# Five engine queues in a new searched order, with register reads as tasks of their own

## The chip, the core and the metric

The kernel runs on one core of a Trainium2 chip. A core has five engines that run side by side, each with an instruction queue that it works off strictly in order: TensorE (PE in the profile, its weight loads apart as PEld), VectorE (DVE), ScalarE (ACT), GpSimd (POOL) and SyncE (SP), which here issues most DMAs. An instruction that waits for another engine holds everything behind it in its own queue. The metric is device time in microseconds (us) of one execution; less is better.

## What is computed

Block-sparse attention (4 batches, 8 heads, 768 positions, head size 64) and then a feed-forward layer with a squared relu on its result:

```python
scores = scale * np.matmul(q, k.transpose(0, 1, 3, 2))
mask = np.abs(blk_i - blk_j) <= window
mask = mask | (blk_i == 0) | (blk_j == 0) | (blk_i == n_blocks - 1) | (blk_j == n_blocks - 1)
for qb in range(n_blocks):
    for kb in sampled_blocks[qb]:
        mask[qb * block:(qb + 1) * block, kb * block:(kb + 1) * block] = True
scores = np.where(mask, scores, -1000000000.0)
attn = np.exp(scores - np.max(scores, axis=-1, keepdims=True))
attn = attn / (np.sum(attn, axis=-1, keepdims=True) + 1e-09)
attn_out = np.matmul(attn, v)
...
h = x @ w_in
r = np.maximum(h, 0.0)
g = r * r
return (g @ w_out).astype(np.float32)
```

x is the attention's output as 3072 rows of 512; w_in is 512 x 2048 and w_out 2048 x 512. A block has 32 positions, there are 24 blocks, and each block of queries sees its neighbours, the first and the last block, and three blocks drawn at random that are only known when the kernel runs.

## The kernel before

Two heads make a unit (u), so there are 16 units, four to a batch. Batches 0 and 1 are computed dense: `scores`, then `exps` on ACT, `masks` on DVE (a product with a 0/1 tile) and `values` on PE, for 256 queries and two key chunks at a time. Batches 2 and 3 are computed sparse, in six visits (v) of two query groups (g) each: `k_gather` copies the keys of the sampled blocks together (on POOL or DVE), `v_gather` and `v_window` fetch their value rows by DMA, and `s_scores`, `s_exps`, `s_masks`, `s_values`, `s_normalize` follow. `s_transp` or `x_transp_dma` turn the result into the x tile of the feed-forward layer. There, `hidden` makes 1024 columns of h in four parts on PE, `relu` (ACT or DVE) and `square` (ACT, or POOL) follow, and `output` multiplies by w_out in eight parts; `out_copy` and `store` bring the result out. `cast_qk` and `cast_v` turn loaded values into bf16 on DVE or POOL.

All of this is cut into some 1200 tasks. A task names the tasks that it depends on (`deps`), the buffers that it takes (`get`) and those that it gives back (`put`); a buffer may be taken again when all who hold it have put it. The string `PROGRAM` is a list of words such as `V120`, `G73` or `P84/1`: the engine (P, V, A, G, S for PE, DVE, ACT, POOL, SP), the task's number and, for tasks that take one of the four PSUM cells X, the cell. `run_program` goes through the words and issues each task's instructions on the engine named. So the string sets which engine does a task and the order in each engine's queue, and nothing else does; waits between engines follow from deps and buffers.

Where the block numbers are needed as addresses (`k_gather`, and `v_gather` where SP issues it), they have to be in registers of the engine that uses them. `blocks_of` (line 559) reads the six numbers of a group with one register load, `load_blocks(e)` (line 569) does it for every group that the program gives to engine e, and `table_rows` (line 523), a short DVE task, calls it for POOL, DVE and SP at once. A `v_gather` on POOL is one indirect DMA (line 579); on SP it is six DMAs with addresses from registers (line 582).

An x tile (pool xT, four buffers) is read by four `hidden` groups of a tile of 256 tokens; before, it is put by the last part of the group with the highest column numbers.

Of the kernel before, what the change touches and what calls it, by code (L numbers as in the profile page):

```python
# [25 lines left out]
def kernel(  # L26
# [14 lines left out]
    nb = S // block  # L41
# [7 lines left out]
    NF = d_ff // P  # L49
# [733 lines left out]
    def T_(f, *args, **kw):  # L783
        return Task((lambda e: f(*args, e)), **kw)
# [146 lines left out]
    tb, mk_claims, mk_buf = {}, [], {}  # L931
# [6 lines left out]
    tb["slots"] = T_(table_slots, deps=[t, p], get=tmp)  # L938
    hb = Buf("X")
# [4 lines left out]
    for us in [range(b * HP, (b + 1) * HP) for b in range(B)]:  # L944
# [11 lines left out]
        if us[0] >= SB * HP:  # L956
            b = us[0] // HP
# [8 lines left out]
    for T in TILES:  # L966
# [3 lines left out]
        for f in range(0, NF, n_u):  # L970
# [31 lines left out]
        A29 G35 P4/3 V32 P30/0 P12/2 P14/3 P9/1 P5/1 V31 P33/1 V111 P36/3 P0/2 A37 V1 V34 P102/2 V209 V46 P47/0 P106/1 A103 V48 P104/3  # L1002
        V43 A107 P44/0 G57 P7/2 V45 A105 P58/1 V54 P113/0 V59 P55/2 A114 P117/3 G41 V56 P2/1 V67 A118 P115/2 V3 P108/0 A116 V64 P127/1
        V109 P10/3 P65/3 A128 P123/2 V66 A124 P68/1 P125/3 G75 V69 V63 P92/1 P110 A126 P133/2 G76 V112 A134 P137/3 G52 S28 S42 S18 S19
        V93 S20 P88/0 A138 G38 V155 V89 P84/1 P119/2 G74 V85 A60 P86/0 P39/3 P135/1 V120 G73 A87 V40 A136 P121 P61/0 G49 P129/3 V122
        V62 G77 V70 P176/2 P170/0 P139/1 A177 G81 V130 G80 A171 V140 P146/2 P131 V132 A147 P149/3 V172 P71/0 P141 V142 A150 V72 P50/2
        P173/1 V148 P781/0 A174 P782 V178 P189/3 P783 V51 A190 V175 P90/1 P15/2 P96/2 P784 V91 A97 P183/3 V151 A785 P94/2 P179/1 V95
        A184 G787 P143/0 P774/2 V180 P775 A144 V191 G78 P186/3 P181 P776 V182 A187 P777 V145 P157/0 V778 A786 P152/3 A158 P160/1 V188
        P788/2 A161 V153 P163/0 P789 V185 A164 P790 V162 P154 P217/1 P791 A156 V159 A218 P192/0 V165 P795/3 A792 V193 S82 P166/1 S83
        V296 V219 S53 S254 A779 G794 S253 P194 P100/2 A780 P796 V195 V167 A101 P214/0 P797 G793 A215 P168 P798 V169 P211/2 V799 P824/1  # L1010
        G79 A212 P825 P196/0 G256 V216 P826 A197 P199/3 P818/2 G801 S257 P827 A200 P819 V828 P202/0 A800 S261 P228/3 P820 G22 A203
        S262 P821 V213 P812/1 S269 A229 V822 P813 G258 P220/0 A829 P814 V201 P245/2 S259 P221 A246 V198 P815 P802/3 V222 A816 P231/2
        V266 P223 P803 A232 V204 S267 P239/1 V230 P804 A224 A240 V264 S270 P242/0 P205/2 V233 S265 A243 P225/1 P206 P805 V207 A226
        S277 V274 P288/0 S436 S255 P208 P806 V227 A289 S275 V247 P11/1 P291/1 A823 P234/0 V241 P807 A292 V210 V244 P98/2 P235 V272
        P808 A99 V236 A817 S273 P298/2 V290 P248/1 P237 A299 P809 V238 S278 V293 P285/0 S279 V300 P249 A810 P830/2 V250 P831 A286 V282
        P304/3 P251 P832 V260 A305 P301/0 V252 P833 S263 V287 P852/1 A302 S334 S283 V834 P853 P846/3 G280 P313/0 V303 P854 A314 P316/2
        S281 P855 P847 A317 V856 G284 P294/0 P848 A835 S271 P295 V306 P310/1 S21 P849 G268 V297 A311 P864/2 V318 P865 S440 A850 P307/0
        V315 P866 S438 A857 P308 G851 S446 P355/3 P867 V309 A356 P322/1 V868 P858/0 P859 A323 P349/3 V357 P325/2 P860 A350 V312 P861
        P836/1 V276 A326 V351 S456 P319/3 A862 P328/2 V327 S439 P320 S447 A329 V321 P352/0 P837 S811 V324 A353 S454 P339/2 V330 P838
        A340 V354 P331/3 P342/0 A869 S385 V341 P332 P358/2 V333 P839 A343 V23 S335 G441 P359 A863 P336/3 P361/0 G443 P840 A337 P841  # L1020
        G451 A362 S622 P364/3 G449 P842 A365 P373/0 G445 S450 P843 A374 G461 P870/3 A844 S444 P367/0 V338 P871 A368 V344 S463 P872
        V347 V360 S455 V366 S442 P376/0 P345/1 A377 V363 P379/2 P346 P873 S452 V348 A380 V369 P403/0 P874 A404 V375 S464 P370/2 V378
        P400/1 P393/0 V381 P371 A401 P875 V372 S471 S448 A394 V402 P382/1 P390/2 V405 P383 A391 P387/0 P876 V384 A388 V395 S386 P406/1
        P886/2 V392 A407 P887 V457 P427/0 P877 A428 V465 P24/1 P888 S497 S462 A878 G453 P889 V408 S458 P880/0 A890 P881 P430/3 S466
        P882 V27 G891 A431 P883 P409/2 A884 P926/3 V26 P927 A885 P410 G469 P415/0 V398 V25 P928 V411 G467 A416 P892/1 S608 V389 P424/2
        S879 P893 A425 P929 S468 V432 P894 A930 P895 V426 P396/0 S470 A896 P16/2 V429 P898/3 S845 P397 S616 A931 P418/2 P433/1 V399
        P899 V459 A419 P932/0 P933 V474 S460 P412/2 P900 A413 P901 V417 P934 A902 S473 P434 V420 P935 V435 P482/3 G903 P904/2 A483
        V936 A897 P492/1 P905 V414 A493 P914/3 G503 P915 P480/0 S499 S623 P421/1 A481 P916 S542 P422 P906 G472 V423 V484 P907 S437
        G937 P917 P487/1 P908 V918 A488 P477/1 P490/0 P909 G501 A478 V504 A491 P485/1 P920/3 A919 G543 V494 P921 V479 V621 P475/0 P910
        A486 G500 V489 V625 A476 P911 V613 P495/1 A912 G546 S632 S913 V547 P511/2 S607 P505/0 V496 P922 A512 S520 S502 P923 A506  # L1030
        P954/1 V924 G627 P955 P514/2 P508/0 P956 A515 V507 G524 P557/3 S545 P957 V513 A509 P948/2 A925 P949 S614 P938/0 G544 A558 S498
        P939 V516 A958 V525 P551/3 S523 P950 A552 P940 V510 P554/3 P951 A555 P548/1 P941 G589 S628 A549 P517/3 A952 P966/1 G959 V518
        A953 P967 P535/2 P942 V550 S519 A536 P529/3 P943 G521 S626 V559 P526/2 P944 V590 G522 A527 P945 V537 P968 V609 A946 P960/2
        P961 V556 A530 P969 V528 P532/0 P962 A970 S540 S615 V553 P963 S585 G586 S624 P988/3 A971 V964 P989 P560/1 A533 V531 P990 A965
        V534 P594/2 P994/0 V561 A595 P995 P991 G567 S562 P996 A992 P538/1 V619 V568 S631 A993 P597/3 P972/2 S606 V539 A598 P997 V596
        S541 P600/1 P973 A601 G587 P1000/3 A998 V617 S620 P974 G999 P975 S610 P572/1 P1001 A573 S630 P982/0 G637 P1002 S588 P1003
        P575/1 P983 V1004 A576 P976 V611 P984 P578/1 P569/3 P985 V629 S612 A570 P977 V599 A986 V633 P978 S563 G565 S618 A579 V602
        P1034/3 A1005 P591/0 G635 V574 S634 P979 A592 P1035 G564 S638 P1028/1 A980 V593 P1036 S566 V580 P1029 A987 P1037 P1030 S639
        S636 V1038 P603/2 P1022/0 V604 P1023 P643/3 P1031 V577 P1024 V571 A1032 P1006/2 V642 S641 A644 P1025 G1033 P1007 V1026 P655/3
        P648/1 P1008 A656 S947 A649 P650/3 P1009 S583 S667 G640 A1039 P581/1 A1027 G671 P645/0 P1010 V582 A651 A646 P658/3 V657 G668  # L1040
        P1011 S584 V652 A659 V672 P653/1 P1012 S605 V647 P660/0 P1016/3 A661 G692 P1017 S688 A654 V662 P1013 P1018 V693 P1019 P663/0
        A1020 A1014 P679/3 P1050/1 V664 S731 S665 S981 A680 P682/2 P1051 S1015 A683 P1062/0 S734 P1063 A1021 V684 P676/3 P1052 S751
        S691 P673/2 A677 P1053 G714 P1064 A674 V1054 P1065 P1040/3 A1066 G669 V715 S670 P1041 A1055 G1067 P700/0 V678 P1042 A701
        P697/1 P1056/2 A698 S690 P694/0 P1043 G689 A695 V681 P1057 P1068/1 V699 P719/0 P1069 V696 A720 P1058 V675 P1070 P1071 S666
        P703/0 P1059 A1072 P1044 V1060 P1045 G1061 P685/2 P716/1 P1046 V686 A704 S710 G711 A717 P1047 V702 S687 G757 A1073 P722/2 G712
        P1074/0 A723 V705 P1075 V1048 P706/2 P725/3 P1076 V707 S753 G754 S713 A726 P1077 V721 G733 V724 S756 P1084/2 V718 P1085 V758
# [42 lines left out]
```

## Time and profile before

| | us |
|---|---|
| median of 3 runs | 259.88 |
| lowest and highest run | 258.5, 267.15 |
| the profiled execution | 258.88 |
| its span on the core | 257.1 |

The profile is of one execution. Its span runs from the first to the last instruction; the 1.8 us between span and time lie outside the instructions. For every instruction it has engine, source line, tiles, start and length, and for idle time before it, which engine's signal ended the wait. The granted TensorE clock was 1.00 in every stage. A tile name such as `X<-xT,w_in_sb` is output, arrow, inputs. An engine's name with a q (DVEq, SPq) is its sequencer: register loads, and the issue of DMAs. In a row of a group stand the count, the busy time, the mean in ns, and the idle time before it with what ended it.

### The profile page before, as it was taken

To read this page: it belongs to the slowest core of one execution; us is meant where nothing else is said; L and a number is where in the kernel's file an instruction comes from. 1 tells how busy PE (TensorE), PEld (TensorE's weight loads), DVE (VectorE), ACT (ScalarE), POOL (GpSimd) and SP (SyncE) were. 2 spreads that over 40 slices of the span, in tenths; PEclk is the share of its full clock that TensorE was granted. 3 is DMA by queue.
4 is the path that set the end of the run, shared out by engine and by line. 5 is a ranking of instruction groups with operands and counts; after the bars stand their busy time and mean duration, and the time that the engine had idled before them with its cause. 6 is when DMAs were issued, how large, how long until landed. Compare 5 with 4: busy or idle time off the path is not lost.

```text
span 257.1 us, 12061 instructions
## 1 busy us (share of the span) xinstructions
PE 243.1 (95%) x5265; PEld 182.1 (71%) x5265; DVE 171.3 (67%) x408; ACT 183.6 (71%) x217; POOL 98.8 (38%) x178
## 2 busy tenths in 40 slices
PE   7888999999999997998998999999999999999993
PEld 4667879678874677975864867866875677767683
DVE  7778988899889995969916756657536725730301
ACT  3899999998999797846783975675965286623640
POOL 3183247003316026198556314264357620412100
PEclk9999999999999999999999999999999999999999
DMA  6999989999999996999699779998474923044022
GB/s 200 374 250 207 206 205 155 270 202 252 250 281 179 197 202 153 340 229 154 188 243 202 194 174 167 251 214 199 129 206 95 189 40 60 5 121 148 23 86 83
DMA packets 64692, 47.08 MB, mean 183 GB/s; under 512 B 31567, under 2 KB 60624, under 8 KB 64640
## 3 DMA queue, kind: packets, MB, share of 16 engines
q1 hardware_dynamic: 58512, 37.82, 64.7%
q0 software_dynamic: 5440, 8.05, 16.8%
q8 instruction: 41, 0.67, 1.1%
q10 hardware_dynamic: 688, 0.46, 0.6%
q14 instruction: 11, 0.09, 0.1%
HBM read 35.51 MB, written 7.91 MB: 169 GB/s over the span
## 4 chain that ended last, share of the span: by engine, by line
PE 53%; DVE 5%; DVEq 1%; issue 1%; ACT 1%; ACTq 0%
PE X L203 49%; PE X L653 4%; DVE VB L123 1%; ACT pT L623 1%; DVEq L561 1%; DVE MKS L123 1%; DVE pT L630 1%; DVE r L709 0%; DVE KG L599 0%; DVE qc L123 0%; DVE XS L413 0%; DVE KG L593 0%; DVE XS L662 0%; DVEq L599 0%; DVE rs L410 0%
## 5 line engine op out<-in xcount | busy, mean ns | idle before, releaser
L203 PE MATMUL X<-xT,w_in_sb 64*128 64x256 bf16 x1536 | 100.8, 269 | 2.8 <-issue 1.5
L203 PE MATMUL X<-w_out_sb,g 64*128 64x512 bf16 (+3 forms) x960 | 95.2, 334 | 0.1
L203 PEld LDWEIGHTS <-w_in_sb 64*128 64x128 bf16 x1536 | 74.6, 94 | 16.0 <-issue 5.4
L360 ACT ACTIVATE pT<-X 128x1024 bf16<-128x1024 f32 x72 | 70.6, 1030 | 7.6 <-PE X L203 6.8
L623 ACT ACTIVATE pT<-X 128x768 bf16<-128x768 f32 (+1 forms) x56 | 41.6, 766 | 26.5 <-PE X L203 23.9
L203 PEld LDWEIGHTS <-g 64*128 64x128 bf16 x960 | 40.3, 94 | 26.3 <-PE X L203 0.4
L720 POOL TENSOR_TENSOR g<-r 128x1024 bf16<-128x1024 f32 (+1 forms) x20 | 31.6, 1587 | 64.4 <-ACT r L707 47.2
L707 ACT ACTIVATE r<-X 128x1024 f32<-128x1024 f32 x28 | 29.8, 1068 | 20.6 <-PE X L203 20.5
L709 DVE TENSOR_SCALAR r<-X 128x1024 f32<-128x1024 f32 x20 | 24.5, 1224 | 26.7 <-PE X L203 13.7
L367 DVE TENSOR_TENSOR pT<-pT,VG 128x1024 bf16<-128x1024 bf16 x60 | 40.9, 715 | 0.2
L718 ACT ACTIVATE g<-r 128x1024 bf16<-128x1024 f32 (+1 forms) x40 | 35.2, 899 | 2.7 <-DVE r L709 2.5
L203 PE MATMUL X<-QKT 64*128 64x256 bf16 (+1 forms) x384 | 31.6, 250 | 3.3 <-DVE XS L413 1.3
L630 DVE TENSOR_TENSOR pT<-pT,MKS 128x768 bf16<-128x768 bf16 (+1 forms) x48 | 27.6, 607 | 10.7 <-ACT pT L623 10.5
L203 PEld LDWEIGHTS <-QKT 64*128 64x128 bf16 x384 | 16.7, 95 | 9.5 <-issue 4.1
L579 POOL DMA_INDIRECT VG<-rows,idx x19 | 20.2, 1061 | 4.4 <-issue 2.6
L203 PEld LDWEIGHTS <-pT 64*128 64x128 bf16 x768 | 16.0, 94 | 1.9
L203 PE MATMUL X<-VB,pT 64*128 64x65 bf16 x768 | 17.1, 190 | 0.0
L203 PEld LDWEIGHTS <-KG 64*128 64x128 bf16 x528 | 13.8, 95 | 4.5 <-issue 0.2
L659 DVE RECIPROCAL ss<-X 128x8 f32<-128x8 f32 x12 | 2.5, 206 | 19.5 <-PE X L653 17.3
L653 PEld LDWEIGHTS <-pT 128*64 128x64 bf16 x624 | 11.9, 111 | 4.9 <-issue 3.7
L203 PE MATMUL X<-QKT,KG 64*128 64x64 bf16 x528 | 15.3, 190 | 0.1
L123 POOL CAST VB<-vs 128x768 bf16<-128x768 f32 x9 | 7.8, 869 | 16.5 <-DMA vs<-in_v_dram 16.4
(107 smaller groups left out, 210.3 us busy)
## 6 DMA issues: line engine op xcount, KB each, us to landing
vs<-in_v_dram SPq DMA_DIRECT2D x14, 384.0 KB
ks<-in_k_dram SPq DMA_DIRECT2D x13, 384.0 KB
qs<-in_q_dram SPq DMA_DIRECT2D x12, 384.0 KB
out_dram<-ys SPq DMA_DIRECT2D x9, 512.0 KB
VG<-rows SPq DMA_DIRECT2D x20, 132.0 KB
w_in_sb<-in_moe_w_in_dram POOLq DMA_DIRECT2D x4, 512.0 KB, 8.6
w_out_sb<-in_moe_w_out_dram POOLq DMA_DIRECT2D x4, 512.0 KB, 9.9
rows<-VB SPq DMA_DIRECT2D x2, 792.0 KB
```

The source lines that it names most:

```text
L123: (V if e == "DVE" else G).tensor_copy(out=out, in_=in_)
L203: last = nc.tensor.matmul(out(r ^ crossed), lhsT(r ^ crossed, rows), rhs(r ^ crossed, rows), skip_group_check=True, **kw)
L360: A.activation(out=pT[:, :, 0:n], in_=stile.pop(a)[:, :, 0:n], func=AF.Exp, scale=scale)
L367: V.tensor_tensor(out=pT, in0=pT, in1=m[:, None].broadcast_to([P, 2, len(cs), w]), op=AOP.mult)
L579: G.indirect_dma_start(out=to[0:RS * HB], out_offset=None, in_=pairs, in_offset=bass.IndirectOffsetOnAxis(ap=idx[0:RS * HB, g - 1:g], axis=0))
L623: A.activation(out=pT[:, :, 0:n], in_=stile.pop((u, v, gs))[:, :, 0:n], func=AF.Exp, scale=scale)
L630: V.tensor_tensor(out=pT, in0=pT, in1=m[:, None].broadcast_to([P, 2, n]), op=AOP.mult)
L653: nc.tensor.matmul(po[i * D:(i + 1) * D, h, a * VW:(a + 1) * VW], pts[g][:, h, c * D:(c + 1) * D], val, start=a == 0 and c == 0, stop=c == ...
L707: A.activation(out=to, in_=src, func=AF.Relu)
L709: V.tensor_scalar(out=to, in0=src, scalar1=0.0, scalar2=None, op0=AOP.max)
L718: A.activation(out=g, in_=r, func=AF.Square)
L720: (G if e == "POOL" else V).tensor_mul(out=g, in0=r, in1=r)
```

## The change

Three edits of code and a new table.

- `table_rows` no longer reads block numbers. `load_blocks(g0, g1, e)` is a task of its own, two for each of POOL, DVE and SP: groups 0 to 3, and the others. Each depends on `table_slots`, which writes the table that is read, and is placed by the program like any other task.
- The x tile is put by the last part of each of its four `hidden` groups, so it is free when all four are done, in whatever order they stand.
- `PROGRAM` is another string, with six more words. Work moves between engines too: ten `cast_qk` from DVE to POOL, seven `square` from ACT to POOL (six of 1024 columns, one of 512), two `relu` from DVE to ACT, five `v_gather` from POOL to SP, one `mask_evac` and one `x_evac` from ACT to DVE and one `evac` (a copy to QKT) the other way. PE has the same tasks.

```diff
@@ table_rows @@
         V.tensor_scalar(out=idx, in0=low[1][:, P:P + GR], scalar1=float(HB), scalar2=lane, op0=AOP.mult, op1=AOP.add)
-        load_blocks("POOL")
-        load_blocks("DVE")
-        load_blocks("SP")
@@ load_blocks @@
-    def load_blocks(e):
-        for g in wanted[e]:
+    def load_blocks(g0, g1, e):
+        for g in [g_ for g_ in wanted[e] if g0 <= g_ < g1]:
             if g not in held_at[e]:
                 held_at[e][g] = blocks_of(g, ENGINE[e])
@@ the list of tasks @@
     tb["slots"] = T_(table_slots, deps=[t, p], get=tmp)
+    for e_ in ("POOL", "DVE", "SP"):
+        T_(load_blocks, 0, 4, deps=[tb["slots"]])
+        T_(load_blocks, 4, nb, deps=[tb["slots"]])
@@ hidden @@
-                             put=[xb[b, c0]] if f + n_u == NF and end else []))
+                             put=[xb[b, c0]] if end else []))
@@ PROGRAM @@
-        A29 G35 P4/3 V32 P30/0 P12/2 P14/3 P9/1 P5/1 V31 P33/1 V111 P36/3 P0/2 A37 V1 V34 P102/2 V209 V46 P47/0 P106/1 A103 V48 P104/3
...
+        G302 A35 V117 P0/0 P9/1 G18 S34 P5/2 P2/3 V1 V3 V38 G41 P42/1 P36/2 A43 A19 V37 P12/0 G52 P39/3 P4/0 G161 P53/1 P15/2 V49 G63
...
```

Task numbers from 24 on are six higher in the new table, and source lines behind `table_rows` are three lower. Three places show what the table does.

The start, on DVE, behind the instruction that writes bm (the block mask, from which PE makes the mask rows R). qc is a cast tile of keys or queries, QKT their transposed form, ks and KG are loaded keys, X the PSUM cells. Before:

```order
L249 TENSOR_SCALAR bm<-r_82 24x2x24
L123 CAST qc_108<-ks_77 128x384
L123 COPY QKT<-X_146 128x2x3x64
L123 CAST R_206<-X_148 128x256
L123 COPY QKT<-X_147 128x2x3x64
L123 CAST qc_109<-qs_75 128x256
```

And now:

```order
L249 TENSOR_SCALAR bm<-r_82 24x2x24
L123 CAST R_206<-X_146 128x256
L123 CAST R_206<-X_149 128x512
L123 CAST qc_107<-ks_77 128x384
L123 COPY QKT<-X_148 128x2x3x64
L123 CAST qc_106<-ks_78 128x768
```

Both casts of R stand first, and the cast of the second half of the first keys (384 columns) behind them; one query cast and one QKT copy have gone to POOL and ACT.

The register reads, on DVE, with the last mask products of the dense batches (L367), the mask tile of the sparse ones (MKS) and a normalize (L410, L413). Before:

```order
L367 TENSOR_TENSOR pT_87<-pT_87,VG_208 128x1024
L123 CAST MKS<-X_147 128x5x64 x3
L123 CAST MKS<-X_147 128x6x64 x3
L524 TENSOR_SCALAR idx<-X_147,lane 128x11
L561 TENSOR_LOAD tab x6
L410 RECIPROCAL rs<-X_148 128x4
L413 TENSOR_TENSOR XS<-X_148,rs 128x2x2x64
```

Now two of the six stand some 30 rows earlier, right behind the table's slots, and four here, among the mask products (L627) and the normalize (L656, L659) of the first sparse visit:

```order
L627 TENSOR_TENSOR pT_91<-pT_91,MKS 128x2x192
L627 TENSOR_TENSOR pT_86<-pT_86,MKS 128x2x192
L558 TENSOR_LOAD tab x4
L656 RECIPROCAL ss<-X_147 128x8
L659 TENSOR_TENSOR XS<-X_147,ss 128x2x4x64
L123 CAST qc_109<-ks_77 128x384 x2
L590 COPY KG_118<-QKT 128x4x64
```

The four reads moved behind that visit's products and ahead of its normalize and of a key gather (L590).

POOL in the dense batches, from the table's last constants (lane) to the second batch's values (VB). A product g<-r is a square. Before:

```order
L474 IOTA lane 32x1 x4
L123 CAST qc_108<-qs_74 128x768
L123 CAST qc_106<-ks_78 128x768
L123 CAST VB_191<-vs_80 128x2x6x64
L123 CAST VB_191<-vs_79 128x2x6x64
L720 TENSOR_TENSOR g_103<-r_81 128x1024
L123 CAST qc_107<-ks_77 128x384 x2
```

And now:

```order
L474 IOTA lane 32x1 x4
L717 TENSOR_TENSOR g_99<-r_83 128x1024
L123 CAST qc_108<-ks_77 128x768
L123 CAST qc_106<-qs_74 128x768
L717 TENSOR_TENSOR g_101<-r_82 128x1024
L123 CAST VB_191<-vs_80 128x2x6x64
L123 CAST qc_107<-ks_77 128x384 x2
L717 TENSOR_TENSOR g_103<-r_81 128x1024
L717 TENSOR_TENSOR g_105<-r_83 128x1024
```

Where one square of 1024 columns stood, there are four now.

More of the change, by code (lines that the diff above doesn't have):

```diff
@@ L1006 @@
[L1006 to L1017, printed above, removed]
@@ new lines @@
+        S268 S267 A103 A791 V157 A190 P100/3 V101 P185/2 P149/1 P780/3 V197 V186 P781 A150 P192/0 P187 P782 V191 P163/1 P783 V188
+        P794/2 A193 A164 V151 V784 A792 P158/0 V159 P166/1 P795 P169/3 P160 A167 A170 P796 V194 G793 P797 V162 V165 V168 P223/1 V171
+        P801/0 P198/3 A224 A798 V199 P172/1 G786 P200 V201 G800 G799 V173 A785 P802 P220/2 P106/3 P803 P174 A107 P804 P217/3 V175 A221
+        A218 P830/1 P831 P202/2 P832 V215 V805 P208/0 V225 P824/3 P825 G806 P833 A807 V222 A203 G262 V264 V834 P826 P205/2 P827 S263
@@ new lines @@
+        S283 V293 G278 A311 S281 S279 S284 V312 P858/0 P859 A840 V286 S285 A308 P322/2 G288 S269 G841 P319/3 P860 A442 P861 S289 G290
+        P852/1 P853 V862 S445 A323 A320 P300/2 P854 P301 P361/3 V309 A863 P316/0 A317 V303 P855 S21 V274 A856 P870/2 S287 P391 V318
+        P313/0 P871 P314 P872 S277 A362 V321 P328/1 P873 V315 V363 P355/3 V874 S452 V324 S446 A329 P864/0 V330 P865 V282 A356 G447
+        P331/1 P866 A332 V333 P867 S503 P334/2 A868 P842/3 P325/1 G857 S453 G869 S462 S444 G451 P11/0 G455 A335 G467 P358/0 S448 P326
@@ new lines @@
+        A1094 P1109 P765/2 S738 P1085 P759 V735 A1095 P1110 S715 A766 P768/1 P746/2 P1111 P1086 A1101 S762 A769 A747 P771/1 S736 G760
+        V751 P1087 P1124/2 A772 A1112 P1125 V1088 P1131/1 S761 S739 S740 P743/3 P1126 A744 V748 V767 V773 P1132 P1114/0 S1055 G1113
+        P1127 P774/3 P1133 A1128 V745 P1115 P1134 P1145/2 V754 A775 V770 P1116 S1089 P1117 P755/3 V1135 V776 G1129 P777/1 V778 P1146
+        P1118 V756 A1130 P1138/1 P1139 P1147 P1140 P1152/3 S758 P1148 V1149 G1151 A1136 A1137 P1153 P1141 A1150 P1119 S779 V1142
@@ L1057 @@
+        P13/0 P6/1 S1209 S1229 S1219
     """
```

83 lines of the change are left out of this document (41 added, 42 removed).

## The prediction

> **What bounds the kernel now.** I read the page first, then the busy time of every engine by stage, then who waited for whom, and last the chain of waits and the timeline at the places that the change touches.
>
> ```profile
> span 257.1 us, 12061 instructions
> PE 243.1 (95%) x5265; PEld 182.1 (71%) x5265; DVE 171.3 (67%) x408; ACT 183.6 (71%) x217; POOL 98.8 (38%) x178
> ```
>
> TensorE (PE) is busy for 95% of the span, so an order can win at most the 14.0 us in which it is idle. The next view says where those lie; its columns are the stretch, its length, and the busy time of PE, PEld, DVE, ACT and POOL.
>
> ```profile
> 0.00:20.00 20.00, 16.34 (x312) 12.11 (x314) 15.06 (x44) 14.59 (x17) 9.38 (x25) 1.00 0.95 272
> 20.00:100.00 80.00, 77.52 (x1719) 60.64 (x1716) 70.30 (x153) 75.55 (x84) 24.16 (x36) 1.00 1.11 217
> 100.00:150.00 50.00, 46.30 (x1088) 35.95 (x1089) 36.72 (x99) 33.73 (x42) 27.91 (x55) 1.00 0.93 207
> 150.00:250.00 100.00, 99.72 (x1988) 70.39 (x1986) 48.46 (x113) 59.41 (x75) 37.36 (x63) 1.00 0.59 134
> 250.00:257.10 7.10, 3.22 (x168) 2.98 (x165) 0.72 (x2) 0.27 (x1) 0.00 (x0) 1.00 0.23 76
> ```
>
> PE is idle for 3.66 us at the start (20.00 - 16.34), 2.48 from 20 to 100, 3.70 from 100 to 150, 0.28 from 150 to 250 and 3.88 in the tail. In the long last stage nothing is left to win. From 20 to 100 ScalarE (ACT) is busy for 75.55 of 80 us and VectorE (DVE) for 70.30: three engines run close to full there, and the shortest work list decides nothing by itself. From 100 to 150 no other engine is full; there it is single waits.
>
> ```profile
> PE X L203 <- issue: 1.7, 5, 0.4
> PE X L203 <- DVE XS L413: 1.3, 2, 1.0
> PE X L653 <- issue: 0.6, 2, 0.4
> ...
> POOL qc L123 <- PE X L203: 17.0, 1, 17.0
> DVE ss L659 <- PE X L653: 17.3, 8, 5.1
> ```
>
> The first three rows (engine and line, what it waited for, us in total, times, longest) are PE's. "issue" is a wait for nothing that the profile shows: 2.3 us in 7 waits, which no order of tasks is known to remove. The longest wait of PE for another engine is 1.0 us for a DVE normalize, and the chain of waits tells what delayed that one:
>
> ```profile
> 95.23 0.40 DVEq L561
> ...
> 98.18 0.94 DVEq L561
> ...
> 100.91 12.49 PE X L203 x318
> ```
>
> L561 is the read of block numbers into registers, six of them in a row on DVE's queue, with the normalize behind them and PE behind that.
>
> **The change part by part.**
>
> Start: DVE now casts both parts of R (the mask rows) ahead of the second half of the first keys, and PE makes both mask rows first.
>
> ```profile
> 4.15 0.17 DVE L249 TENSOR_SCALAR bm<-r 24x48 bf16<-24x48 f32 x1
> 4.58 0.55 DVE L123 CAST qc<-ks 128x384 bf16<-128x384 f32 x1 [0.25 <-DMA ks<-in_k_dram]
> 5.04 0.35 DVE L123 COPY QKT<-X 128x384 bf16<-128x384 bf16 x1
> 5.79 0.42 DVE L123 CAST R<-X 128x256 bf16<-128x256 f32 x1 [0.40 <-PE X L258]
> 6.93 2.85 ACT L360 ACTIVATE pT<-X 128x1024 bf16<-128x1024 f32 x3 [0.88 <-PE X L203]
> ...
> 11.19 0.67 DVE L123 CAST R<-X 128x512 bf16<-128x512 f32 x1
> ```
>
> bm is there at 4.32; a mask row's matmul takes some 0.3 (estimate), so the two R casts run from about 4.8 to 5.9 (0.42 + 0.67), then the key cast to 6.4 and the first QKT copy to 6.75. The first exp can start near 7.3 instead of 6.93. It was followed by a hole until the second unit's keys came, and the 0.67 of the R cast is gone from 11.19, where ACT ran without holes. I take +0.3; ends -0.5 (the 0.67 saved and the start hidden) and +0.8.
>
> ACT from 20 to 100: up to the copy of the third output tile, ACT loses three full squares, a half one, a mask and an x copy, and gains two relus and a QKT copy.
>
> ```profile
> L718 ACT ACTIVATE g<-r 128x1024 bf16<-128x1024 f32 x25 | 26.5, 1063 | 0.1
> L718 ACT ACTIVATE g<-r 128x512 bf16<-128x512 f32 x15 | 8.8, 626 | 2.6 <-DVE r L709 2.5
> L707 ACT ACTIVATE r<-X 128x1024 f32<-128x1024 f32 x28 | 29.8, 1068 | 20.6 <-PE X L203 20.5
> L277 ACT ACTIVATE VG<-X 128x512 bf16<-128x512 f32 x4 | 2.4, 607 | 0.0
> L709 DVE TENSOR_SCALAR r<-X 128x1024 f32<-128x1024 f32 x20 | 24.5, 1224 | 26.7 <-PE X L203 13.7 <-POOL g L720 10.2 <-POOL KG L599 1.6
> L720 POOL TENSOR_TENSOR g<-r 128x1024 bf16<-128x1024 f32 x11 | 21.6, 1968 | 36.0 <-ACT r L707 24.2 <-DVE r L709 11.7
> ```
>
> That is -3 x 1.06 - 0.63 - 0.61 + 2 x 1.07 = -2.3 us (the two small copies cancel). PE can take back no more than its 2.48 idle there, and part of that is DVE's. Ends 0 and -2.3; I take half, -1.2, since no engine alone sets the pace.
>
> Register reads: the rows of L561 give their number and length.
>
> ```profile
> L561 DVEq TENSOR_LOAD <-tab x6: 857/992/1067, 93.8 to 99.2; - x6
> L561 POOLq TENSOR_LOAD <-tab x5: 774/973/1096, 95.9 to 100.0; - x5
> L561 SPq TENSOR_LOAD <-tab x3: 712/727/1343, 97.7 to 99.9; - x3
> ```
>
> On DVE two of the six now follow the table's slots, among masks; four stand behind the mask products of visit 0 and ahead of its normalize. The 1.0 us of PE's wait goes: -1.0 (ends 0, if another step of DVE is as late, and -1.3, both waits of that row). The four, 4 x 0.99 = 4.0 us, are covered by the values of that visit, for which DVE has waited anyway (17.3 us in 8 waits, row above). If that cover is gone, the next key gather on DVE comes up to 4.0 us late and PE's scores of visit 3 with it. SP reads eight instead of three: 5 x 0.73 = 3.6 us more ahead of a transpose and of the first window of visit 0; the visit's scores were moved later, so I take 0, with an end at +1.0.
>
> 100 to 150: DVE has three relus fewer by the first visit's normalize (3 x 1.22 = 3.7 us) and casts fewer keys and queries. Of PE's 3.70 idle, 1.0 is counted above and up to 2.3 is issue; so some 0.4 to 1.1 can follow. I take -0.5; ends 0 and -1.1.
>
> POOL: ten casts and seven squares (six full, one half) come to it, five gathers leave. A full square takes 1.97 there (row L720) against 1.06 on ACT, so POOL gets 6 x 1.97 + 1.1 + casts of 0.6 to 1.3 each, less five gathers of about 1 us: some 17 us more, on an engine idle for 62% of the span. Its own time is hidden by that idleness (17.0 us in the one wait shown). What it does to DVE is not hidden:
>
> ```profile
> L367 DVE TENSOR_TENSOR pT<-pT,VG x60: 679/684/1240, 22.3 to 109.9; 128x1024 bf16<-128x1024 bf16 x60
> 113.89 1.90 POOL L720 TENSOR_TENSOR g<-r 128x1024 bf16<-128x1024 f32 x1
> 114.06 1.97 DVE L630 TENSOR_TENSOR pT<-pT,MKS 128x384 bf16<-128x384 bf16 x1
> ```
>
> A mask product takes 0.68 in the median and 1.24 at most, and the small one at 114.06, of 384 columns against 1024, lasted 1.97: it ended at 116.03, just after the square on POOL (115.79). I price a meeting at 0.56 (1.24 - 0.68) for a cast and 1.4 for a square. DVE's idle time (9.7 us of 80) and the work taken from it cover most; I take +0.4, ends 0 and +6.4 (the slower rival's).
>
> The Trainium skill, SBUF — State Buffer, section "Who interferes with whom", says that a DVE instruction with two SBUF inputs and a GpSimd instruction that reads SBUF exclude each other: the later one waits for the whole instruction. The row at 114.06 agrees: 1.97 us beside a square of 1.90. By that rule every moved square may hold a mask product for its full length, and the sum would end with the slower rival below; by the median row (0.68, so most products met nothing) it stays as I have it.
>
> Gathers: five more go by SP, six register moves and DMAs each.
>
> ```profile
> L582 SPq MOVE VG<-rows x18: 29/29/38, 190.4 to 217.0; - x18
> L582 SPq DMA_DIRECT2D VG<-rows x18: 315/315/1072, 190.5 to 217.1; - x18
> ```
>
> 30 x 0.34 = 10 us of SP's queue, nearly all behind 150 us, where PE has 0.28 idle. Behind them wait x transposes and stores; PE has whole hidden tiles of other visits to do, so 0, with an end at +1.5. The x tiles given back by their last reader only allow hidden units in any order: 0.
>
> Tail: two pieces of keep-warm matmuls leave the last output's matmuls and stand behind them: -0.2 (0 to -0.4), an estimate from the rows of the last stage.
>
> Sum: +0.3 - 1.2 - 1.0 - 0.5 + 0.4 - 0.2 = -2.2. The profiled execution took 258.88, 1.78 beyond its span; 258.88 - 2.2 = 256.7 us. The median of the runs, 259.88, lies 1.0 above the profiled one.
>
> **The rivals.**
>
> No change, 258.9 (258 to 260): PE's own work is the same to the instruction, and a hole filled at one place opens at the next when three engines run nearly full. For it: the sums are small beside 257. Against it: the 1.0 us wait has a named cause that moves.
>
> A larger gain, 253.3: all of ACT's 2.3, DVE's 1.3 and 1.1, the tail's 0.4 and the start's -0.5 come, -5.6 in all. For it: ACT is 94% busy in the long stage. Against it: each term would have to reach its end at once.
>
> Slower, 265.3: POOL's new work holds DVE's mask products between 20 and 100 us, where the values on PE wait for masks. Three more full squares stand there (four instead of one) and at least four more casts; if each meets a product and nothing covers it, that is 3 x 1.4 + 4 x 0.56 = +6.4. It decides from the point where such holds exceed the work that DVE lost (3.7 us of relus and some casts) and its idle time at the place. For it: the row at 114.06. Against it: the median of 0.68, and DVE's 9.7 us of idle time in that stage.
>
> **How the numbers follow.** Forecast 0.48, no change 0.22, larger gain 0.17, slower 0.13. The likeliest case alone spans 254.7 to 258.5. The range 252.5 to 261.5 holds the first three and, of the slow one, the part in which fewer than half of the holds meet. A measurement of this kernel can tell about 2% from no change; that is below 253.7 or above 264.1 against 258.88. Faster takes the larger gain and 0.03 of the forecast, 0.20; slower nearly all of its rival, 0.12; within, the rest, 0.68.
>
> **What would show it.** The first exp near 7.3 us. No L561 in the chain of waits, and the normalize before 100 us with no wait of PE for XS. PE idle from 20 to 100 near 1.3 us, from 100 to 150 near 2.2. The mask product's median still near 0.68, with its longest ones more often beside POOL squares. The last stage still without idle time. It is wrong if PE's idle time in 20 to 150 grows above 6.2, if the mean of the masks rises by more than 0.1 us, or if waits for gathers landing by SP show up behind 150 us.

## The result: slower by 5%, and the profile after

| | us |
|---|---|
| changed kernel, median of 4 runs (270.28 to 277.84) | 273.52 |
| kernel before on the same chip, median of 4 | 260.04 |
| ratio, with its 95% interval | 1.052 [1.040, 1.065] |

The profile shown is that of the changed kernel run once more, beside the first experiments: an execution of 274.45 us. In that set of runs the changed kernel takes 1.057 [1.045, 1.069] of the kernel before. First the page's head:

```profile
span 272.3 us, 12176 instructions
PE 246.3 (90%) x5265; PEld 185.9 (68%) x5265; DVE 183.7 (67%) x393; ACT 178.0 (65%) x211; POOL 124.6 (46%) x194
```

POOL has 25.8 us more work than before, ACT 5.6 less. DVE was given less to do and is busy for 12.4 us more. The busy time by stage (same columns as before the change; the last three are the granted clock of PE, the share of the DMA engines and GB/s):

```profile
0.00:20.00 20.00, 15.91 (x299) 12.06 (x300) 13.91 (x38) 14.12 (x18) 10.51 (x26) 1.00 0.90 264
20.00:100.00 80.00, 71.54 (x1572) 54.95 (x1570) 68.88 (x139) 66.20 (x73) 38.58 (x46) 1.00 1.02 206
100.00:150.00 50.00, 43.18 (x952) 33.48 (x950) 29.25 (x83) 32.35 (x39) 27.96 (x43) 0.93 0.93 200
150.00:250.00 100.00, 97.09 (x2062) 71.39 (x2055) 68.81 (x134) 57.43 (x71) 44.48 (x78) 1.00 0.59 137
250.00:272.30 22.30, 18.60 (x410) 13.96 (x404) 2.88 (x3) 7.92 (x12) 3.08 (x3) 1.00 0.23 73
```

PE is idle for 8.46 us from 20 to 100 (2.48 before), 6.82 from 100 to 150 (3.70) and 2.91 from 150 to 250 (0.28). That is 11.7 us more idle time, and the clock is below 1 in the third stage, where it was 1.00. What PE waited for, from the view of waits (us in total, times, longest):

```profile
PE X L203 <- DMA QKT<-qc: 5.1, 2, 4.8
PE X L203 <- DVE pT L367: 4.0, 3, 2.4
PE X L203 <- DMA w_in_sb<-in_moe_w_in_dram: 1.8, 3, 0.9
```

None of the three stood in that view before. The first is the transposed keys of unit 11, for which PE waits up to 129.8 us; the next view shows what SP did ahead of that transpose (register reads as a group, then the timeline of SP):

```profile
L558 SPq TENSOR_LOAD <-tab x8: 712/716/1502, 113.8 to 121.2; - x8
```

```profile
111.81 1.92 SPq L312 DMA_TRANSPOSE QKT<-qc  x1
119.94 0.40 SPq L151 DMA_DIRECT2D ks<-in_k_dram  x1
120.44 0.72 SPq L768 DMA_DIRECT2D out_dram<-ys  x1
122.48 0.38 SPq L151 DMA_DIRECT2D ks<-in_k_dram  x1
122.95 1.52 SPq L312 DMA_TRANSPOSE QKT<-qc  x1
```

From 113.8 to 119.9 SP reads registers, seven times. Then it works off what stood behind them, an eighth read at 121.2 among it, and the transpose goes out at 122.95. The second wait has the same kind of cause on DVE. The chain of waits:

```profile
87.42 1.46 DVEq L558
88.95 1.37 DVEq L558
90.41 0.19 DVE pT L367
```

Two register reads stand right behind the table's slots, and the mask products behind them come 3 us later. Last, the mask products themselves, DVE's largest work, in the view of groups (busy us, mean ns; then idle time ahead of them):

```profile
L367 DVE TENSOR_TENSOR pT<-pT,VG 128x1024 bf16<-128x1024 bf16 x60 | 47.6, 833 | 4.2 <-ACT pT L360 4.2
L627 DVE TENSOR_TENSOR pT<-pT,MKS 128x768 bf16<-128x768 bf16 x40 | 28.7, 748 | 2.4 <-ACT pT L620 2.3
L627 DVE TENSOR_TENSOR pT<-pT,MKS 128x384 bf16<-128x384 bf16 x8 | 8.8, 1134 | 6.9 <-ACT pT L620 6.9
```

and in the kernel before:

```profile
L367 DVE TENSOR_TENSOR pT<-pT,VG 128x1024 bf16<-128x1024 bf16 x60 | 40.9, 715 | 0.2
L630 DVE TENSOR_TENSOR pT<-pT,MKS 128x768 bf16<-128x768 bf16 x40 | 23.3, 613 | 10.7 <-ACT pT L623 10.5
L630 DVE TENSOR_TENSOR pT<-pT,MKS 128x384 bf16<-128x384 bf16 x8 | 4.4, 577 | 0.0
```

The same 108 products take 85.1 us instead of 68.6. What the longest one looks like, on the timelines of DVE and of POOL:

```profile
185.74 4.04 DVE L627 TENSOR_TENSOR pT<-pT,MKS 128x384 bf16<-128x384 bf16 x1 [2.97 <-ACT pT L620]
```

```profile
185.80 3.76 POOL L717 TENSOR_TENSOR g<-r 128x1024 bf16<-128x1024 f32 x2
```

A product that takes 0.34 us undisturbed (the shortest of these rows) lasts 4.04, across two squares on POOL.

To compare many kernels, two sums are worked out from each trace. *PE's waits*: the time from one matmul's start to the next beyond what is usual for its shape (0.108 us for 512 columns, 0.054 for 256), a slower clock included; the span is this sum plus 231 us in every kernel here, within 0.8. *Held*: for every mask product and key copy on DVE the time beyond its undisturbed length, counted from the end of the instruction ahead where the two overlap (so 0.60, 0.47 and 0.27 us for the three products, 0.20 and 0.10 for the copies).

```
                     ratio to before          PE's waits, us, by stretch                       held
                     (95% interval)           0-20  20-100  100-150  150-200  200-   sum       us
before               1                         6.2     7.1      8.1      2.4    1.9  25.7       9.7
changed kernel       1.057 [1.045, 1.069]      6.7    14.1     12.1      5.7    2.6  41.1      31.9
e5  SP reads         1.047 [1.041, 1.052]      6.6    11.9      8.8     10.7    4.6  42.7      26.8
e6  DVE reads        1.038 [1.034, 1.043]      6.7    10.7     11.1      5.0    4.5  38.0      33.3
e7  weights          1.045 [1.038, 1.052]      7.2    11.8     11.8      5.6    4.7  41.0      31.9
e8  all three        1.038 [1.030, 1.046]      7.3    11.0      6.1      5.9    3.6  33.7      35.3
e9  short squares    1.038 (two runs)          7.0     9.6     10.9      2.7    5.5  35.6      11.7
e10 before, short    0.998 [0.994, 1.001]      6.8     6.5      5.4      1.9    1.5  22.1      10.4
e11 e8 and short     1.017 [1.011, 1.023]      6.2    11.5      7.7      2.7    4.2  32.2      16.9
e12 e8, ACT squares  1.040 [1.034, 1.045]      5.9    12.1      5.5      6.8    4.8  35.2      19.7
e13 squares alone    1.032 [1.025, 1.038]      6.4    12.7      9.5      6.8    3.0  38.4      23.3
e14 gathers alone    1.031 [1.024, 1.038]      6.9     8.4     10.7      2.8   10.1  38.9       9.0
e15 DVE reads alone  1.005 [0.999, 1.010]      7.7    11.8      8.0      2.8    2.9  33.4       9.0
e16 e8, late gathers 1.032 [1.023, 1.040]      6.2    11.8      5.9      6.6    5.7  36.0      35.0
e17 reads behind     1.003 [0.998, 1.008]      6.2     9.0      8.5      1.8    1.8  27.3       9.8
e18 two squares      1.008 [1.004, 1.013]      6.5     8.7      9.1      2.8    1.8  28.9       6.9
```

The ratios leave out executions that took over 1.5% more than their kernel's fastest (six of twelve for e15 and eight of twelve for e17, where the medians of all are 1.012 and 1.014 of before), and the sums are of one execution each, from 2 us below its kernel's median (e8) to 4 above (e11).

### The profile page after: what moved, and what is told of

Same layout as the page of the kernel before. It is cut to its first block, busy times and chain, and to the rows that moved or that the text cites. A ratio compares the mean times of both kernels' runs of the same rounds, so it can differ in the third digit from the quotient of the medians.

```text
span 275.7 us, 12176 instructions
## 1 busy us (share of the span) xinstructions
PE 246.8 (90%) x5265; PEld 185.7 (67%) x5265; DVE 187.0 (68%) x393; ACT 178.0 (65%) x211; POOL 122.9 (45%) x194
## 4 chain that ended last, share of the span: by engine, by line
PE 33%; DVE 20%; DMA 18%; SPq 10%; issue 8%; ACT 6%; POOL 2%; DVEq 1%; ACTq 0%; POOLq 0%
PE X L203 29%; DVE pT L367 7%; DMA w_in_sb<-in_moe_w_in_dram 5%; DMA VG<-rows 4%; PE X L650 3%; ACT pT L360 3%; DVE KG L596 3%; SPq L558 2%; DMA QKT<-qc 2%; DVE pT L627 2%; DMA qs<-in_q_dram 2%; SPq L579 2%; DMA ks<-in_k_dram 2%; SPq L663 2%; DVE r L706 2%
## 5 line engine op out<-in xcount | busy, mean ns | idle before, releaser
L203 PE MATMUL X<-w_out_sb,g 64*128 64x512 bf16 (+3 forms) x960 | 97.2, 337 | 1.2 <-DVE XS L659 1.1
L717 POOL TENSOR_TENSOR g<-r 128x1024 bf16<-128x1024 f32 (+1 forms) x27 | 45.5, 1691 | 67.7 <-ACT r L704 41.6
L367 DVE TENSOR_TENSOR pT<-pT,VG 128x1024 bf16<-128x1024 bf16 x60 | 47.1, 824 | 4.1 <-ACT pT L360 4.1
L704 ACT ACTIVATE r<-X 128x1024 f32<-128x1024 f32 x30 | 31.8, 1065 | 23.9 <-PE X L203 23.8
L627 DVE TENSOR_TENSOR pT<-pT,MKS 128x768 bf16<-128x768 bf16 (+1 forms) x48 | 36.1, 787 | 10.4 <-ACT pT L620 7.3
L715 ACT ACTIVATE g<-r 128x1024 bf16<-128x1024 f32 (+1 forms) x33 | 28.4, 873 | 18.1 <-DVE r L706 18.0
L706 DVE TENSOR_SCALAR r<-X 128x1024 f32<-128x1024 f32 x18 | 22.0, 1220 | 10.1 <-PE X L203 9.8
L576 POOL DMA_INDIRECT VG<-rows,idx x14 | 14.0, 1000 | 15.9 <-DMA rows<-VB 9.5
L123 POOL CAST qc<-ks 128x384 bf16<-128x384 f32 (+1 forms) x17 | 12.0, 728 | 17.7 <-DMA QKT<-qc 10.3
L596 DVE COPY KG<-QKT 128x64 int32 x72 | 18.8, 332 | 0.0
L656 DVE RECIPROCAL ss<-X 128x8 f32<-128x8 f32 x12 | 2.5, 205 | 19.9 <-PE X L650 19.9
```

Of the source, the lines that this page charges most:

```text
L123: (V if e == "DVE" else G).tensor_copy(out=out, in_=in_)
L203: last = nc.tensor.matmul(out(r ^ crossed), lhsT(r ^ crossed, rows), rhs(r ^ crossed, rows), skip_group_check=True, **kw)
L367: V.tensor_tensor(out=pT, in0=pT, in1=m[:, None].broadcast_to([P, 2, len(cs), w]), op=AOP.mult)
L576: G.indirect_dma_start(out=to[0:RS * HB], out_offset=None, in_=pairs, in_offset=bass.IndirectOffsetOnAxis(ap=idx[0:RS * HB, g - 1:g], axis=0))
L596: eng.tensor_copy(out=rows[:, :, :, r_ * w:(r_ + 1) * w], in_=src[:, :, :, bass.ds(at[r_] * w, w)])
L627: V.tensor_tensor(out=pT, in0=pT, in1=m[:, None].broadcast_to([P, 2, n]), op=AOP.mult)
```

## The experiments

The theories, by the letters of the expectations: H, POOL's new work holds DVE's products; S, register reads and gathers on SP stand ahead of transposes that PE needs; D, two reads on DVE stand ahead of mask products; W, the weights come late; O, none of these alone, the new order is worse as a whole.

### Giving moved work back to its old engine (e1 to e4)

The changed kernel unchanged; all 29 squares and 20 casts whose engine the table had changed on their old engine again; the five gathers on POOL again (SP reads three registers, not eight); both.

```diff
 e2: the words of 29 square, 20 cast_qk and cast_v tasks
-  G..   (or A.., V..)
+  the engine of the kernel before, at the same place in the list
 e3: v_gather 2 1 1, 3 2 0, 3 3 0, 3 3 1, 3 4 1
-  S..
+  G..
```

> The changed kernel as it is, to have its time beside the others and a second profile. Every theory: 270 to 274 us, ratio about 1.05. Theory H (POOL's longer work holds DVE): the longest DVE products and key copies again lie beside a POOL square or cast, and the 60 dense mask products take over 800 ns in the mean. Theory S (SP's register reads and gathers): the transpose behind the seven register reads on SP again ends late, and PE waits over 3 us for it near 125 us.

> In the changed kernel, every square and every cast of q, k, v is done by the engine that did it before (POOL back from 27 to 20 squares and from 24 to 14 casts of q and k); nothing changes place in the list. Theory H: at least half of the 13 us loss comes back, 261 to 266 us, and DVE's dense mask products fall back to about 720 ns in the mean. Theory S: at most 2 us come back. Rival O (the order as a whole, with no single cause): between 0 and 4 us come back and other waits appear.

> In the changed kernel, the five value gathers that moved from POOL to SP are POOL's again, so SP reads three groups of block numbers instead of eight and issues 30 DMAs fewer. Theory S: 4 to 7 us come back (3.4 of the wait for keys near 125 us, 2 to 3 of waits for gathered values behind 230 us), 264 to 268 us. Theory H: 0 to 2 us, since POOL gets five gathers more and DVE is held as before.

> Both undone: squares, casts and the five gathers as before, the rest of the new order kept. H and S together: 258 to 262 us, as the kernel before. Rival O: still over 265 us, because the loss lies in the order of each queue and not in what moved between engines.

Measured: 272.80, 284.14, 270.79 and 286.18 us (before 259.79), ratios 1.057, 1.097 [1.083, 1.112], 1.049 [1.038, 1.060] and 1.109 [1.098, 1.121]. The expectation that work given back brings time back fell. In e3 no wait of PE for the keys of unit 11 is left, but S had 4 to 7 us for it, and its ratio can't be told from that of the changed kernel. In e4 a cast on POOL waited 20.5 us for its keys with all else of POOL behind it, and at four tasks PE lost 2.8 to 4.1 us. A task put on another engine at its old place can block that engine's queue, so e2 and e4 don't tell what the holds are worth. From here on either single words were moved on their own engine, or the cost itself was taken away.

### Moving the named waits away (e5 to e8)

```diff
 e5, SP
    transp_dma 10 0
-   load_blocks 4 nb
    load 14 1
 ...
    load 12 0
    ...
+   load_blocks 4 nb
    s_transp 2 1
 e6, DVE
    table_slots
-   load_blocks 0 4
 ...
+   load_blocks 0 4
    normalize 4 512
 e7, POOL: weight loads
-   1 6 0 2 3 7 4 5
+   1 0 2 3 6 7 4 5
```

> The changed kernel; SP's seven register reads (0.72 us each) move from ahead of the transpose of unit 11 (113 us) to ahead of the transpose of s_normalize 2 1 (146 us), where SP waits for 3.5 us; all else as it is. S (the reads in front of the transposes make PE wait 5.1 us at 129.8, and the clock falls to 0.83 for some 8 us after it): about 272.8 - 5.1 - 1.5 = 266, no wait of PE over 1.5 us for the keys of unit 11. H (POOL holds DVE) and O (the order has many small faults, so a hole closed here opens at the next): 270 to 273, with the 5 us back within 30 us.

> The changed kernel; DVE's two register reads (1.3 us each) move from right behind the table's slots (87 us) into the gap ahead of the last normalize of visit 1 (108 to 112 us), where DVE waits for PE for 3.7 us. D (the reads hold three mask products and with them the values of unit 4 on PE, 2.6 us at 92.4, and the clock at 90 to 100): 272.8 - 2.6 - 1.0 = 269. H and O: 271 to 273.

> The changed kernel; the eight weight loads in the order 1 0 2 3 6 7 4 5 instead of 1 6 0 2 3 7 4 5, so that the four parts of w_in, of which the first hidden units wait, go ahead of the parts of w_out. W (the late w_in costs 2.4 us at 32 to 36 us, hidden units 0, 8 and 12): 270.5. H and O: 272 to 273, the waits at 32 to 36 us gone and others in their place.

> The three moves together. If named waits add up: 272.8 - 6.6 - 3.6 - 2.4 = 260, level with the kernel before (259.8). If POOL's holds on DVE are the main cause (H), they are all still there, and no more than 5 us come: 268 or more. If the order as a whole is worse (O): between 264 and 268, with PE idle from 20 to 100 us still above 5 us.

e5: the wait for the keys of unit 11 is gone (100 to 150 us: 8.8 instead of 12.1), but the ratio is only 0.01 lower, with intervals that overlap. In the profiled execution, which took 3.3 us more than e5's median, another wait took its place at 166 us:

```profile
PE X L203 <- DVE XS L659: 3.2, 1, 3.2
```

a normalize. It stood behind a cast of values on DVE, which waited 5.0 us for its load and then, beside a square and a cast on POOL, took 3.38 us, where casts of this shape take 0.97 in the mean in the kernel before. Whether e5's other executions lose their gain at the same place isn't shown. e6 did best: 269.49 us, as D had it, and 1.038, clear of the changed kernel's interval. No wait over 1.2 us is left from 55 to 125 us, and the wait for the keys of unit 11 is 2.7 us. e7: the waits for w_in are gone and PE waits 2.3 us less from 20 to 100, but the sum of its waits is the same and the ratio can't be told from that of the changed kernel; whether W is worth its 2.4 us isn't settled. All three together are no better than e6 alone: 268.77 against 259.25 before, where named waits that add up would have made it 260. S and D are real waits, but they don't add up to the loss; H or O hold the rest.

### Taking the holds away (e9 to e12)

A hold needs a long square on POOL. Instead of moving it, three kernels make it short:

```diff
-            (G if e == "POOL" else V).tensor_mul(out=g, in0=r, in1=r)
+            G.memset(g, 0.0)
+            G.tensor_mul(out=g[:, :64], in0=r[:, :64], in1=r[:, :64])
```

> The changed kernel, with each square on POOL cut to a fill of its tile with zeros (writes only) and the square of its first 64 columns; 27 squares are left out for the most part, their places, waits and followers are the same. H (POOL's squares hold DVE's mask products and key copies, beyond their median lengths by some 21 us in the trace of the changed kernel): 272.8 less 6 to 10 = 263 to 267, and the products lose most of those 21 us. O (the order as such, the holds lie in idle time of DVE): 270 or more, though the holds are gone from the trace.

> The kernel before, with its 20 squares on POOL cut in the same way. H: its squares hold DVE for 3.6 us in all, so little is to be won: 258 to 260. If a short square helps any order (POOL's own 1.9 us on the way to the outputs, or the zeros in the matmuls), it falls as much as the changed kernel does: 250 to 254, and what the changed kernel wins says nothing of holds.

> The changed kernel with the three moves (reads of SP and DVE, weight loads) and with the short squares. If reads and holds together are the cause: 268.8 - 6 to 9 = 260 to 263, within 1.5% of the kernel before with short squares. O: 266 or more.

The fourth gives nine squares between 140 and 195 us to ACT.

> The changed kernel with the three moves, and nine of POOL's squares between 140 and 195 us (units (1,512) 0, 8, 12; (2,0) 12; (2,256) 0, 4, 8, 12; (2,512) 8) done by ACT, in place in its list; ACT is busy for 54 of the 100 us there. H: the holds behind 140 us fall from 19 to some 6 us, 268.8 - 2 to 4 = 265 to 267. If ACT's squares (1.06 each) delay the exps behind them as much: 268 to 270. O: 268 to 269.

The products of e9, in the view of groups:

```profile
L367 DVE TENSOR_TENSOR pT<-pT,VG 128x1024 bf16<-128x1024 bf16 x60 | 41.9, 737 | 3.9 <-ACT pT L360 3.9
L627 DVE TENSOR_TENSOR pT<-pT,MKS 128x768 bf16<-128x768 bf16 x40 | 21.0, 568 | 4.9 <-ACT pT L620 4.8
L627 DVE TENSOR_TENSOR pT<-pT,MKS 128x384 bf16<-128x384 bf16 x8 | 2.6, 366 | 9.4 <-ACT pT L620 9.4
```

The holds fall to 11.7 us from 31.9, about what the kernel before has (9.7), and PE's waits from 150 to 200 fall from 5.7 to 2.7, about what they were before the change. The time of e9 settles less: its median is 269.37 us, and the two executions that enter the ratio take 264.29 and 267.84, 1.038 of before. H's 263 to 267 meant 1.012 to 1.028 of the 259.8 before, O's 270 meant 1.039, and two executions can't decide between them. The wait for the keys of unit 11 (4.9 us at 125) is still there. With the reads moved too (e11) the ratio is 1.017, against 1.038 for the same kernel with full squares (e8): 5.4 us, with intervals apart. In the kernel before the same cut wins 0.2%, within its interval, and leaves the holds at 10.4 us. So with the reads out of the way the short squares are worth some 5 us. A missed part: e11 was to be within 1.5% of the kernel before with short squares (e10), and is 2.0% behind it.

A short square does two more things than to end a hold. It feeds the matmuls zeros, and it lets POOL's next task start earlier. e10, with 20 such squares, shows that neither wins anything in the order before. In the changed order the second isn't tested apart; in e8 PE's one wait for POOL is 0.6 us for a key copy, and none is for a square.

e12 missed: the holds behind 150 us fell from 19 to 5 us, but the time didn't (1.040 against 1.038). So where in the span the 5 us lie stays open. At 192 us PE now waits for ACT, where the square went:

```profile
PE X L203 <- ACT g L715: 2.0, 1, 2.0
```

### One part alone in the order before (e13 to e16)

Three kernels have the order of the kernel before and one part of the change; the fourth is e8 with the last two gathers of SP on POOL.

```diff
 e13: 29 squares
-  the engine of the kernel before
+  the engine of the changed kernel, in the old place
 e14: v_gather 2 1 1, 3 2 0, 3 3 0, 3 3 1, 3 4 1
-  G..
+  S..
   SP
+  load_blocks 4 nb
+  load_blocks 0 4
   transp_dma 11 0
 e15, DVE
   table_slots
+  load_blocks 0 4
 ...
   table_rows
-  load_blocks 0 4
-  load_blocks 4 nb
 ...
+  load_blocks 4 nb
   k_gather 2 3 7
 e16: v_gather 3 5 1, 3 4 1
-  S..
+  G..
```

> The order of the kernel before, with the engines of the squares alone as in the changed kernel (29 squares change between ACT and POOL, 27 on POOL instead of 20), each in its old place. H as a property of the engine choice: the holds on DVE's products and key copies rise from 9.7 us to over 20 and the time by 3 to 6 us over before. If the holds come from where the order puts the squares against the products: the holds rise to some 15 us and the time by 0 to 2 us.

> The order of the kernel before, with the five gathers on SP as in the changed kernel and SP's eight register reads ahead of the transpose of unit 11. S (reads in front of a transpose that PE needs): +1.5 to +5 us, with a wait of PE for the keys of unit 11. If SP has time there: 0, within 1 us; then the 5 us at 129.8 in the changed kernel come from its order, in which that transpose was issued late.

> The order of the kernel before, with two of DVE's six register reads behind the table's slots and four ahead of the gather of the fourth window's keys. By the prediction's step: -1.0 us, the wait of PE for the normalize at 100.9 gone. D (two reads behind the slots hold the mask products queued there): PE waits for values near 87 us, 0 to +2.5 us.

> The changed kernel with the three moves, and the last two gathers by SP (3 5 1 and 3 4 1) given back to POOL, so that the window of visit 3 4 is issued behind no gather. If SP's late gathers are the wait of 1.7 to 2.1 us at 230: 268.8 - 1.5 to 2.5 = 266.5. If PE then waits at the same place for something else: 268 to 269.

e13 takes 268.74 us against 260.43: +3.2%, beyond H's 3 to 6 us. The holds rise from 9.7 to 23.3 us, as H had it, and PE's waits in every stretch from 20 to 200 us. Not all of the 8 us are holds: eleven squares came to ACT in exchange, and at 126 us PE waits 2.3 us for an exp, ahead of which ACT stood idle for 5.2 us for something that the profile doesn't name.

e14 takes 269.27: +3.1%, with no more holds than before (9.0). Here S holds, with more than its 1.5 to 5 us, at two places. For the keys, between 116 and 122 us, and for x tiles, between 207 and 229:

```profile
PE X L203 <- DMA QKT<-qc: 2.8, 1, 2.8
...
PE X L203 <- DMA xT<-XS: 4.9, 2, 3.5
```

SP's timeline has the reason for the second:

```profile
197.75 6.81 SPq L579 DMA_DIRECT2D VG<-rows  x12
204.67 1.26 SPq L663 DMA_TRANSPOSE xT<-XS  x1
206.20 3.79 SPq L579 DMA_DIRECT2D VG<-rows  x6
210.09 1.20 SPq L663 DMA_TRANSPOSE xT<-XS  x1
```

The transposes of the x tile stand behind 18 DMAs of gathers, which take 10.6 us, 0.59 each. The profiled execution took 2 us more than e14's median.

e15: 1.005 [0.999, 1.010], where the prediction's step had -1.0 us. The wait of PE at the normalize is gone and another stands at the values near 89 us, right behind the two reads (first read at 86.0). The waits of PE from 86 to 90, and DVE's reads:

```profile
PE X L203 <- DVE pT L367: 2.1, 2, 1.9
```

```profile
L558 DVEq TENSOR_LOAD <-tab x6: 805/808/1358, 86.0 to 127.8; - x6
```

It is the place at which the changed kernel waits at 92.4 us, so D's wait is there in the order before too. The net of both moves, +0.5%, can't be told from zero.

e16: 1.032 against e8's 1.038, with intervals that overlap. The wait for the window of visit 3 4 is gone, and the sparse values between 212 and 216 us lose some 2 us instead, in three pieces. Not settled.

### A try to beat the kernel before (e17, e18)

The order before, with DVE's reads behind the normalizes; and this with two squares that hold a product done by ACT.

```diff
 e17, DVE
   table_rows
-  load_blocks 0 4
-  load_blocks 4 nb
 ...
+  load_blocks 0 4
   k_gather 2 0 1
 ...
+  load_blocks 4 nb
   normalize 6 512
 e18: also square (1,256) 12 and (3,0) 12
-  G..
+  A..
```

> The order of the kernel before; of DVE's six register reads two stand right ahead of the first key gather, behind the second normalize of their visit, and four ahead of the last normalize, in the 2.5 us for which DVE waits for PE there. If the wait of PE at 100.9 us was the reads' price: -1.2 us, 0.995 of before, the wait at the scores of unit 7 gone and none at the values near 87 us. If the reads only hold whatever comes next: within 0.5 us of before.

> As the run with the reads behind, and the two squares on POOL that hold a mask product longest in the kernel before, (1,256) 12 and (3,0) 12, done by ACT. If holds cost PE in that order too: another -0.5 to -1.5, 0.990 of before. If DVE's idle time covers them: no more than the run with the reads behind; if ACT's square (1.06 us) now delays an exp, +0.5.

Neither wins: 1.003 [0.998, 1.008] and 1.008 [1.004, 1.013]. In e17 the old wait is gone and a longer one stands between 108 and 114 us, for the key gather behind two reads that take 2.7 and 2.6 us there:

```profile
PE X L203 <- DVE KG L596: 3.6, 1, 3.6
```

In e18 the holds are the fewest of all kernels (6.9 us) and the time isn't less, which fits an order that has its few holds where DVE can spare the time.

## Why the prediction was wrong

Predicted were 256.7 us and "no difference" as likeliest; measured were 273.5. The rival on the slower side named one of the causes, the holds, but at 0.13 and with about half of the loss. The steps that failed are the prices of POOL's new work and of SP's reads and gathers, each taken as covered, and of two of DVE's reads, which got none. Step by step, in the prediction's order:

- **Start, +0.3.** Right in kind, small in size: the first exp starts at 7.64 instead of 7.3, and the waits up to 20 us are 6.7 against 6.2.
- **ACT, -1.2.** ACT did get lighter, but PE could take nothing back: from 20 to 100 PE waits 0.8 us for ACT, 3.1 for mask products and 1.8 for w_in.
- **Register reads on DVE, -1.0.** Half right. The named wait did go (PE's longest for that normalize is 0.3 us now). But the step followed the four reads that moved behind the products and gave no price to the two "among masks". Those were the 2.4 us wait at 92 us. e15 and e17 show that a read on DVE holds whatever stands behind it: three places, three waits.
- **DVE relief, -0.5.** It didn't come. From 100 to 150 PE's idle time rose from 3.70 to 6.82, most of it in one wait.
- **POOL, +0.4.** The largest miss, with the gathers. The median product is still near 0.68, as foreseen, but the mean rose from 715 to 833 ns. POOL's own work grew by 25.8 us where some 17 were foreseen; its casts of 384 query columns take 979 ns in the mean instead of 621, the longest 3.85 us beside DVE's copies and products, so the holds go both ways. The end of +6.4 counted meetings between 20 and 100 us alone; of the 31.9 us held, 20.1 lie behind 150, where the prediction looked at PE's idle time (0.28 before) and not at what an order without meetings was worth. By e8 against e11 the squares' length costs 5 us, by e13 their new engines 8 in the order before.
- **Reads and gathers on SP, 0.** The other large miss. The prediction saw the transposes behind both and took it that PE had other work until then; that cover wasn't there. The reads took the 5 us ahead of the keys of unit 11, and e14 alone costs 8 us in the order before. Behind 150 us the gathers cost the changed kernel little that its profile shows: one wait of 0.3 us. A gather's DMA was priced at 0.34 us, by the median length of the issue; in a row of them they take 0.59.
- **Not in the sum.** The order of the weight loads (W) was left out, and e7 can't tell it from nothing. The clock was left out too: behind a long wait PE runs at half speed for some us (below), so the 5 us wait costs about 8.
- **Tail, -0.2.** PE's idle time in the last stage is 3.70 us instead of 3.88, too little to tell.

"Wrong if" named the signs: PE idle from 20 to 150 above 6.2 us (15.3), the products' mean up by more than 0.1 us (0.118), and waits for gathers behind 150, of which there is the one of 0.3 us.

What is shown: reads and gathers on SP, and the squares' new engines, cost 3% each in the order before; with short squares and with the named reads and the weight loads moved, the changed kernel is within 1.7% [1.1, 2.3] of before. The parts sum to some 17 us where the change costs 13 to 15. Why parts don't add is argued from e5, e8 and e12: where one wait goes, another appears. What stays open is the last 1.7%: in the profiled execution of e11, 4 us above its median, PE still waits 4.4 us longer than before from 20 to 100, in many pieces below 1 us and one of 2.5, and 2.3 us longer behind 200. That a search over orders left out holds and the length of SP's queue would fit all of this, but no run shows what it counted.

## What to carry to other kernels

When work moves to an idle engine, price it by what it does to the neighbours: who shares a port with it and which of its queue's later instructions others wait for; the engine's own idle share says nothing of either. In a tuned order an engine assignment and its place belong together (e4, with everything handed back, was the slowest of all), so test a suspected cost by making it short in place. And measure causes together as well as alone: here each cure by itself brought 0 to 2%, and the next wait often stood right behind it.

## What the runs showed of the hardware

A DVE product can be held by two POOL squares in a row (4.04 us beside 3.76, rows above): the second square, too, ran while the product stood unfinished. The Trainium skill, SBUF — State Buffer, section "Who interferes with whom", says that the other side blocks for the whole instruction; the trace agrees and goes further, since the hold spanned two.

PE's clock falls behind a long wait. In the changed kernel, by stretches around the wait for the keys of unit 11:

```profile
123.00:130.00 7.00, 2.16 (x33) 1.05 (x31) 3.80 (x13) 1.57 (x3) 4.74 (x13) 0.91 1.07 225
130.00:136.00 6.00, 6.00 (x78) 3.28 (x75) 0.63 (x2) 3.85 (x5) 0.89 (x2) 0.53 1.10 253
```

PE is busy for all 6 us from 130 to 136 at 0.53 of its clock, which is some 3 us of work lost beyond the 5 us of waiting. The Trainium skill, TensorE: Matmul & The Clock Gate, section "Part 1: The HAM clock gate", has half clock after an idle window of about 3.4 us; this wait agrees. Shorter ones were followed by half clock too: 2.7 us in e6 (0.52 from 128 to 131) and 2.1 us in e15 (0.51 from 90 to 93.5). Behind the 2.4 us at 92.4 in the changed kernel the clock stayed at 1.00, so here the length of one wait doesn't decide.

A register read of six words has no fixed length: 0.71 us at the least on SP and up to 1.50, 0.80 to 2.67 on DVE (e17), and 0.78 to 2.87 on POOL in the changed kernel.

One execution of e2 took 576.56 us, with a mean 64x256 matmul of the hidden layer at 494 ns, where the changed kernel has 271, and a granted clock of 1.00 in the records. One of e7 took 310.43 us, at a granted clock of 0.76. Both are left out of the ratios, and nothing here explains them.
